# Bursts of the attention's small matmuls, 600 places ahead in the scheduler's order

## The chip, the core and the metric

The kernel runs on one core of a Trainium2 chip. The core has a matrix engine (PE, whose weight loads are listed apart as PEld), a vector engine (DVE), a scalar engine (ACT), GpSimd (POOL), and SyncE (SP), on whose queue most transfers are issued. Each engine works through its own instructions in their order, and they wait for each other through semaphores. The metric is the device time of one execution in microseconds (us); of several executions the median counts. The profile is of one further execution.

## The reference

Three parts follow each other: an attention over 4 batches of 8 heads (576 positions, 64 columns), a gated product of four weight matrices, and a mixture of 8 experts, of which each of the 2304 tokens uses one.

```python
q_d = q.reshape(B, H, Sd, 4, D).mean(axis=3)           # k_d, v_d likewise
out_up = np.repeat(sm_attn(q_d, k_d, v_d), 4, axis=2)
mask = np.abs(pos[:, None] - pos[None, :]) < 4
attn = softmax(where(mask, scale * q @ k.T, -1e9))
x = (out_up + attn @ v).transpose(0, 2, 1, 3).reshape(2304, 512)
...
h = (x @ w1) * (x @ w2) @ w3
x = h @ w_out
...
e_idx = argmax(x @ w_gate); h = maximum(x[mask] @ w1[e], 0); ye = h @ w2[e]
out[mask] = gate_w * sigmoid(x @ w_output_gate)[e] * ye
```

## The kernel before

**Stages.** First `w_out` and `w3` come in as 64-bit numbers, are unpacked to 32 bits by three DVE instructions for each block (`f64_bits`, lines 127 to 129) and multiplied with each other into `wc`, so that only one product follows the gated one. Then `w1` and `w2` are unpacked in the same way (`w_part`), and the tokens go through in six groups of 384: `g1_step` multiplies a group with a 128-column block of `w1` and of `w2` and forms the gated product, `g2_step` multiplies that with `wc`. From the third stage on the experts' products follow; their order on PE is written out by hand (`ordered`).

**Large products.** Each of them is made of three matmuls (`mm3`, lines 390 to 392), since every operand is split in a rounded high part and a remainder, and both are held in the type fp32r. Their moving operands have 256 to 384 columns here.

**The attention.** It is worked in 16 units, a pair of heads each, and has five steps for a unit:
- `a_T`: sums of four neighbours (`qz` on POOL, `kd` on DVE);
- `a_S1`: 24 matmuls of 32x64 (line 191) for the band of local scores and three of 96x144 (line 202, operand `kd`) for the coarse ones; DVE, POOL and ACT form the exponentials;
- `a_S2`: sums, reciprocals and scaling on DVE and POOL (`sm`, `ed`, `vd`);
- `a_V1`: a DVE transpose of `sm` (line 237), four ACT copies of it into `bd` (line 240), and six PE transposes of `ed` (line 245) that ACT copies into `pt`;
- `a_V2`: four matmuls with `pt` (line 256) and twelve with `bd` (line 260), then ACT and DVE add the results into `xr`, from which `x_split` makes `xh` and `xl` for `g1_step`.

The operands of these small matmuls are plain fp32. Each small matmul leaves two records in the trace, a transpose one. Their results go to three PSUM tiles that take turns (`at`).

**What sets the order.** `step(n)` takes the next n attention steps from a list (`side`), and the tables `GSTEP`, `W3STEP`, `G1STEP` and `G2STEP` say how many are taken after which product. All attention steps of a batch must be through before the group that reads them is split. The order in which instructions then stand on each engine is made by a scheduler: an instruction has a priority by its place in the program, and among those that it takes to be ready the one that stands earliest goes first. A step is written inside `tc.high_priority(offset=120)`, so all that it issues stands 120 places earlier than its place in the program:

```python
    def step(n=1):
        for _ in range(n):
            if side:
                fn, u = side.pop()
                with tc.high_priority(offset=120):
                    fn(u)
```

So a burst of small matmuls and the large products around it can stand at nearly the same priority and mix. The transfers for the next units (`a_load`, `a_loadk`, `a_loadd`, `a_loadv`) are issued on SP by `step` behind the steps that free their buffers.

Of the kernel before, what the change touches and what calls it, by code (L numbers as in the profile page):

```python
# [21 lines left out]
B, H, S, D = 4, 8, 576, 64  # L22
# [26 lines left out]
def attention_moe_kernel(ctx: ExitStack, tc: tile.TileContext, q, k, vw_in, v4_in, w1, w2, w3, w_out,  # L49
                         w_gate, w_ogate, e_w1, e_w2, out):  # L50
    nc = tc.nc
# [13 lines left out]
    def mt(shape, dt, name, tag=None, bufs=None):  # L65
        return main.tile(shape, dt, name=name, tag=tag or name, bufs=bufs)


    ident = mt([P, P], F32, "ident")
# [68 lines left out]
    def at(shape, dt, name, bufs=1):  # L138
        return att.tile(shape, dt, name=name, tag=name, bufs=bufs)

    kz = at([P, 2, 584], F32, "kz")
    qTs = [at([P, 584], F32, f"qT{i}") for i in range(2)]
    bd = at([P, 12, 96], F32, "bd")
# [2 lines left out]
        nc.gpsimd.memset(t, 0.0)  # L146
    st = {}

    def a_load(u):
        d = st.setdefault(u, {})  # L150
        qT = qTs[u % 2]
        kc = at([P, S], F32, "kc")
        nc.sync.dma_start(out=kc, in_=k[u])
        nc.sync.dma_start(out=qT[:, 0:S], in_=q[u])
        d.update(kc=kc, qT=qT)
# [28 lines left out]
    def a_S1(u):  # L184
        d = st[u]
        qT = d["qT"]
        ps = psa.tile([P, 512], F32, name="at", tag="at")
        sl = ps[:, 0:384].rearrange("p (b h k) -> p b h k", b=6, h=2)
        for g in range(24):
            b, j = divmod(g, 4)  # L190
            nc.tensor.matmul(sl[32 * j:32 * j + 32, b], qT[:, 24 * g:24 * g + 32], kz[:, :, 24 * g:24 * g + 32],  # L191
                             start=True, stop=True, tile_position=(0, 32 * j))
        sm = at([P, 6, 2, 32], F32, "sm", bufs=2)
        mx = at([P, 6, 2], F32, "mx")
        nc.vector.tensor_tensor(sm, sl, mask.unsqueeze(2).to_broadcast([P, 6, 2, 32]), op=ALU.add)
        nc.vector.tensor_reduce(out=mx, in_=sm, axis=AX.X, op=ALU.max)
        nc.gpsimd.tensor_tensor(sm, sm, mx.unsqueeze(3).to_broadcast([P, 6, 2, 32]), op=ALU.subtract)
        ps = psa.tile([P, 512], F32, name="at", tag="at")
        sd = ps[0:96, 0:432].rearrange("p (q k) -> p q k", q=3)
        qf = qz.rearrange("p h n -> p (h n)")  # L200
        for qb in range(3):
            nc.tensor.matmul(sd[:, qb], qf[:, 96 * qb:96 * qb + 96], d["kd"], start=True, stop=True)  # L202
        ed = at([96, 3, 144], F32, "ed", bufs=2)
        md = at([96, 3], F32, "md")
        nc.vector.tensor_reduce(out=md, in_=sd, axis=AX.X, op=ALU.max)
        nc.vector.tensor_scalar(md, md, -1.0 / 128, None, op0=ALU.mult)
        zd = at([96, 3], F32, "zd", bufs=2)
        nc.scalar.activation(out=sm, in_=sm, func=AF.Exp, scale=0.125)
        for qb in range(3):
            nc.scalar.activation(out=ed[:, qb], in_=sd[:, qb], func=AF.Exp, scale=1.0 / 128,  # L210
                                 bias=md[:, qb:qb + 1], accum_out=zd[:, qb:qb + 1])
        d.update(sm=sm, ed=ed, zd=zd)
# [20 lines left out]
    def a_V1(u):  # L233
        d = st[u]
        sm, ed = d["sm"], d["ed"]
        sT = at([P, 12, 32], F32, "sT")
        nc.vector.transpose(sT, sm.rearrange("p b h k -> p (b h) k"))
        for j in range(4):
            r = slice(32 * j, 32 * j + 32)
            nc.scalar.copy(out=bd[r, :, 24 * j:24 * j + 24], in_=sT[r, :, 0:24])  # L240
        pt = at([72, 2, 288], F32, "pt")
        for kb in range(2):
            pv = psa.tile([P, 512], F32, name="at", tag="at")
            for qb in range(3):
                nc.tensor.transpose(pv[0:72, 96 * qb:96 * qb + 96], ed[:, qb, 72 * kb:72 * kb + 72], ident[0:96, 0:96])  # L245
            nc.scalar.copy(out=pt[:, kb], in_=pv[0:72, 0:288])
        d["pt"] = pt

    def a_V2(u):
        d = st.pop(u)  # L250
        b, hp = divmod(u, H // 2)
        vw, vd, pt = d["vw"], d["vd"], d["pt"]
        xl = [psa.tile([P, 512], F32, name="at", tag="at") for _ in range(2)]
        for kb in range(2):
            for h in range(2):
                nc.tensor.matmul(xl[0][64 * h:64 * h + 64, 288:432], vd[:, kb, h, :], pt[:, kb, 144 * h:144 * h + 144],  # L256
                                 start=(kb == 0), stop=(kb == 1))
        for c in range(6):
            for h in range(2):
                nc.tensor.matmul(xl[c // 3][64 * h:64 * h + 64, 96 * (c % 3):96 * (c % 3) + 96], vw[:, c, D * h:D * h + D],  # L260
                                 bd[:, 2 * c + h, :], start=True, stop=True)
        up = at([P, 144], F32, "up")
        nc.scalar.copy(out=up, in_=xl[0][:, 288:432])
        for a in range(2):
            n = b * S + 288 * a
            assert G * split[0] >= n + 288 - RING
            o = 0
            while o < 288:
                r0 = (n + o) % RING
                w = min(288 - o, RING - r0)  # L270
                nc.vector.tensor_tensor(
                    xr[:, hp, r0:r0 + w].rearrange("p (n r) -> p n r", r=4), xl[a][:, o:o + w].rearrange("p (n r) -> p n r", r=4),
                    up[:, 72 * a + o // 4:72 * a + (o + w) // 4].unsqueeze(2).to_broadcast([P, w // 4, 4]), op=ALU.add)
                o += w
# [5 lines left out]
    for b in range(B):  # L280
        for s in range(UB + 4):
            for lag, fn in ((4, a_V2), (3, a_V1), (2, a_S2), (1, a_S1), (0, a_T)):
                if 0 <= s - lag < UB:
                    side.append((fn, b * UB + s - lag))
    side.reverse()
# [7 lines that stand above are left out]
                if fn is a_V1:  # L293
                    a_loadv(u)
                if fn is a_T and u + 1 < NU:
                    a_load(u + 1)
                if fn is a_S1:
                    if u + 1 < NU:
                        a_loadk(u + 1)
                    a_loadd(u)  # L300
# [580 lines left out]
    for n in range(4):  # L881
        f64_load("3", n)
        if n == 1:
            a_load(0)
            a_loadk(0)
# [212 lines left out]
```

## Time and profile before

| | us |
|---|---|
| three timed runs | 777.54, 775.76, 778.25 (median 777.54) |
| the profiled execution | 771.75 |
| its span, from the first to the last instruction | 769.9 |
| PE busy in the span | 739.4 |
| DVE busy in the span | 436.3 |
| POOL, ACT busy in the span | 322.9, 279.6 |

A busy share says how long an engine had something under way, not whether its work was dense. The records of PE overlap: a matmul's time runs from its start to its modelled end, while the next one has already begun, so its cost is read from start to start. Line numbers are those of the kernel before. The attention and the gated products fill the span up to about 480 us; the experts follow.

### The profile page before, as it was taken

How to read it: one execution, taken by the hardware profiler on the slowest of the kernel's cores; microseconds unless marked ns; L12 is line 12 of the kernel's file. 1: busy time of each engine (PE TensorE's matmuls, PEld its weight loads, DVE VectorE, ACT ScalarE, POOL GpSimd, SP SyncE). 2: the span in 40 equal slices, each digit the busy share in tenths (PEclk: the TensorE clock that was granted, in tenths of full speed). 3: DMA queues.
4: the chain of work that ended last, by engine and by line, in shares of the span. 5: the costliest groups of instructions: out<-in, count | busy, mean ns of one | idle time of the engine just before them, and what ended most of it. 6: DMA issues, size and time to landing. Idle time of an engine off the chain costs nothing.

```text
span 769.9 us, 14699 instructions
## 1 busy us (share of the span) xinstructions
PE 739.4 (96%) x5710; PEld 683.3 (89%) x5711; DVE 436.3 (57%) x940; ACT 279.6 (36%) x624; POOL 322.9 (42%) x306
## 2 busy tenths in 40 slices
PE   5789999999999999999999999989999999999995
PEld 3667987888978898899899999978999999999994
DVE  8977897962653254445324343455765566676731
ACT  3423534550233223323421212045443644544610
POOL 6744576852360125213201112035654656755611
PEclk9899999999999999999999999998999999999999
DMA  9994565542131313121110010256645447447301
GB/s 325 332 240 139 173 189 160 171 136 91 54 109 31 115 29 111 47 77 38 42 42 22 1 42 1 60 199 241 213 146 210 148 149 268 146 148 260 111 23 39
DMA packets 38264, 97.72 MB, mean 127 GB/s; under 512 B 6018, under 2 KB 12930, under 8 KB 38192
## 3 DMA queue, kind: packets, MB, share of 16 engines
q1 hardware_dynamic: 34768, 86.82, 35.1%
q0 software_dynamic: 3424, 9.93, 3.6%
q8 instruction: 46, 0.75, 0.4%
q14 instruction: 26, 0.21, 0.1%
HBM read 84.93 MB, written 12.29 MB: 126 GB/s over the span
## 4 chain that ended last, share of the span: by engine, by line
PE 86%; issue 5%; POOL 3%; DVE 3%; DMA 1%; ACT 1%; SPq 0%; POOLq 0%; ACTq 0%
PE g L390 24%; PE g L392 24%; PE g L391 23%; PE at L260 3%; PE at L191 3%; PE at L256 2%; PE at L202 2%; PE tr L686 1%; PE at L245 1%; PE tr L779 1%; POOL out_dram L769 1%; DMA early<-in_moe_w_dram 1%; PE g L322 1%; POOL W L713 1%; DVE wf L129 1%
## 5 line engine op out<-in xcount | busy, mean ns | idle before, releaser
L390 PE MATMUL g<-xh,W 128*128 128x384 f32 x384 | 133.8, 349 | 0.0
L392 PE MATMUL g<-xh,W 128*128 128x384 f32 x384 | 131.0, 342 | 0.0
L391 PE MATMUL g<-xl,W 128*128 128x384 f32 x384 | 130.8, 341 | 0.0
L713 DVE TENSOR_TENSOR W<-raw,W 128x1024 fp32r<-128x1024 f32 x32 | 87.9, 2780 | 32.2 <-ACT W L711 30.1
L713 POOL TENSOR_TENSOR W<-raw,W 128x1024 fp32r<-128x1024 f32 x29 | 82.8, 2879 | 37.0 <-ACT W L711 37.0
L390 PE MATMUL g<-xT,W 128*128 128x288 f32 (+6 forms) x256 | 82.2, 321 | 1.0 <-ACT xT L690 1.0
L391 PE MATMUL g<-xT,W 128*128 128x288 f32 (+6 forms) x256 | 80.2, 313 | 0.0
L392 PE MATMUL g<-xT,W 128*128 128x288 f32 (+6 forms) x256 | 80.0, 312 | 0.0
L423 POOL TENSOR_TENSOR h<-a,h 128x384 fp32r<-128x384 f32 x30 | 30.7, 1023 | 113.9 <-ACT h L421 113.7
L390 PEld LDWEIGHTS g<-xh,W 128*128 128x128 f32 x384 | 72.2, 188 | 3.2 <-issue 0.4
L392 PEld LDWEIGHTS g<-xh,W 128*128 128x128 f32 x384 | 72.1, 188 | 1.9 <-issue 0.4
L391 PEld LDWEIGHTS g<-xl,W 128*128 128x128 f32 x384 | 72.2, 188 | 1.5 <-issue 0.2
L390 PE MATMUL g<-wc,h 128*128 128x272 f32 (+1 forms) x240 | 70.2, 293 | 0.0
L391 PE MATMUL g<-wc,h 128*128 128x272 f32 (+1 forms) x240 | 70.0, 292 | 0.0
L390 PE MATMUL g<-h,W 128*128 128x288 f32 (+5 forms) x224 | 70.0, 312 | 0.0
L392 PE MATMUL g<-wc,h 128*128 128x272 f32 (+1 forms) x240 | 69.9, 292 | 0.0
L391 PE MATMUL g<-h,W 128*128 128x288 f32 (+5 forms) x224 | 68.1, 304 | 0.0
L392 PE MATMUL g<-h,W 128*128 128x288 f32 (+5 forms) x224 | 68.1, 304 | 0.0
L711 ACT CAST W<-raw 128x1024 fp32r<-128x1024 f32 x61 | 59.8, 1046 | 8.1 <-DMA raw<-in_moe_w_dram 4.3
L419 DVE TENSOR_TENSOR a<-g,a 128x384 f32<-128x384 f32 x48 | 26.7, 556 | 60.2 <-PE g L392 56.4
L739 ACT ACTIVATE h<-g 128x288 fp32r<-128x288 f32 (+6 forms) x64 | 27.9, 436 | 78.6 <-PE g L392 76.3
L390 PEld LDWEIGHTS g<-xT,W 128*128 128x128 f32 x256 | 49.1, 192 | 1.5 <-ACT xT L690 1.4
(255 smaller groups left out, 1721.8 us busy)
## 6 DMA issues: line engine op xcount, KB each, us to landing
raw<-in_moe_w_dram SPq DMA_DIRECT2D x61, 512.0 KB, 3.6
f64w<-in_moe_w_dram SPq DMA_DIRECT2D x16, 512.0 KB
f<-in_moe_w_dram SPq DMA_DIRECT2D x16, 512.0 KB, 6.5
vw<-in_vw_dram SPq DMA_DIRECT2D x16, 384.0 KB, 3.2
kc<-in_k_dram SPq DMA_DIRECT2D x16, 288.0 KB, 6.4
qT<-in_q_dram SPq DMA_DIRECT2D x16, 288.0 KB, 4.3
kz<-in_k_dram SPq DMA_DIRECT2D x32, 144.0 KB, 3.7
v<-in_v_dram SPq DMA_DIRECT2D x16, 288.0 KB
```

Of the source, the lines that this page charges most:

```text
L191: nc.tensor.matmul(sl[32 * j:32 * j + 32, b], qT[:, 24 * g:24 * g + 32], kz[:, :, 24 * g:24 * g + 32], start=True, stop=True, tile_positio ...
L202: nc.tensor.matmul(sd[:, qb], qf[:, 96 * qb:96 * qb + 96], d["kd"], start=True, stop=True)
L256: nc.tensor.matmul(xl[0][64 * h:64 * h + 64, 288:432], vd[:, kb, h, :], pt[:, kb, 144 * h:144 * h + 144], start=(kb == 0), stop=(kb == 1))
L260: nc.tensor.matmul(xl[c // 3][64 * h:64 * h + 64, 96 * (c % 3):96 * (c % 3) + 96], vw[:, c, D * h:D * h + D], bd[:, 2 * c + h, :], start=T ...
L390: nc.tensor.matmul(ps, whi, xhi, start=first, stop=False)
L391: nc.tensor.matmul(ps, whi, xlo, start=False, stop=False)
L392: return nc.tensor.matmul(ps, wlo, xhi, start=False, stop=last)
L419: nc.vector.tensor_tensor(a, pp[1][:, 0:G], a, op=ALU.mult)
L423: eng.tensor_tensor(lo, a, hi.bitcast(F32), op=ALU.subtract)
L711: nc.scalar.copy(out=hi, in_=t)
L713: ins = eng.tensor_tensor(lo, t, hi.bitcast(F32), op=ALU.subtract)
L739: return nc.scalar.activation(out=t[:, 0, 0:C], in_=ps[:, 0:C], func=AF.Relu), nc.vector.scalar_tensor_tensor(t[:, 1, 0:C], ps[:, 0:C], 0. ...
```

## The change

A context `burst()` is added that puts whatever is issued inside it 600 places further ahead. It is laid around the small matmuls of `a_S1` (both kinds), the transposes of `a_V1` and the matmuls of `a_V2`. The offset adds to the 120 of `step`. The matmuls themselves, their operands, the instructions on other engines and the tables are as before; but since the scheduler goes by what is ready, other instructions change places with them.

```diff
+    def burst():
+
+        return tc.high_priority(offset=600)
...
-        for g in range(24):
-            b, j = divmod(g, 4)
-            nc.tensor.matmul(sl[32 * j:32 * j + 32, b], qT[:, 24 * g:24 * g + 32], kz[:, :, 24 * g:24 * g + 32],
-                             start=True, stop=True, tile_position=(0, 32 * j))
+        with burst():
+            for g in range(24):
+                b, j = divmod(g, 4)
+                nc.tensor.matmul(sl[32 * j:32 * j + 32, b], qT[:, 24 * g:24 * g + 32], kz[:, :, 24 * g:24 * g + 32],
+                                 start=True, stop=True, tile_position=(0, 32 * j))
...
-        for qb in range(3):
-            nc.tensor.matmul(sd[:, qb], qf[:, 96 * qb:96 * qb + 96], d["kd"], start=True, stop=True)
+        with burst():
+            for qb in range(3):
+                nc.tensor.matmul(sd[:, qb], qf[:, 96 * qb:96 * qb + 96], d["kd"], start=True, stop=True)
...
-            for qb in range(3):
-                nc.tensor.transpose(pv[0:72, 96 * qb:96 * qb + 96], ed[:, qb, 72 * kb:72 * kb + 72], ident[0:96, 0:96])
+            with burst():
+                for qb in range(3):
+                    nc.tensor.transpose(pv[0:72, 96 * qb:96 * qb + 96], ed[:, qb, 72 * kb:72 * kb + 72], ident[0:96, 0:96])
...
+        with burst():
+            for kb in range(2):
+                for h in range(2):
+                    nc.tensor.matmul(xl[0][64 * h:64 * h + 64, 288:432], vd[:, kb, h, :], pt[:, kb, 144 * h:144 * h + 144],
+                                     start=(kb == 0), stop=(kb == 1))
+            for c in range(6):
+                for h in range(2):
+                    nc.tensor.matmul(xl[c // 3][64 * h:64 * h + 64, 96 * (c % 3):96 * (c % 3) + 96], vw[:, c, D * h:D * h + D],
+                                     bd[:, 2 * c + h, :], start=True, stop=True)
```

Four lines are added ahead of them and one at each burst, so lines 191, 202, 245, 256, 260 and 390 to 392 are 196, 208, 252, 264, 268 and 398 to 400 in the new file.

The order on PE in the second token group's gated products (`g_2772` to `g_2830`), where `a_V2` of the ninth unit stands. Before:

```order
L391 MATMUL g_2772<-xl,W_1618 128x384
L256 MATMUL at<-pt,vd 64x144
L392 MATMUL g_2772<-xh,W_1619 128x384
L256 MATMUL at<-pt,vd 64x144
L390 MATMUL g_2772<-xh,W_1618 128x384
L256 MATMUL at<-pt,vd 64x144
L391 MATMUL g_2772<-xl,W_1618 128x384
L256 MATMUL at<-pt,vd 64x144
L392 MATMUL g_2772<-xh,W_1619 128x384
L260 MATMUL at<-bd,vw 64x96
L390 MATMUL g_2772<-xh,W_1618 128x384
L260 MATMUL at<-bd,vw 64x96
```

Now, the same unit:

```order
L196 MATMUL at<-kz,qT_112 32x64 x13
L264 MATMUL at<-pt,vd 64x144 x4
L268 MATMUL at<-bd,vw 64x96 x6
L398 MATMUL g_2815<-xh,W_1797 128x384
...
L398 MATMUL g_2830<-xh,W_1806 128x384
L268 MATMUL at<-bd,vw 64x96 x6
L252 MATMUL at<-ident,ed 72x96 x6
```

The row before it went on in the same way: sixteen small matmuls stood in fifteen pieces, each behind a large one. Now they stand in two, the first behind another unit's `a_S1`, with nineteen large matmuls between the two.

The order on PE where `a_S1` of the sixth unit stands. Before, in the first group's gated products (`g_1469`):

```order
L191 MATMUL at<-kz,qT_113 32x64
L390 MATMUL g_1469<-xh,W_1356 128x384
L191 MATMUL at<-kz,qT_113 32x64
L391 MATMUL g_1469<-xl,W_1356 128x384
L191 MATMUL at<-kz,qT_113 32x64
L392 MATMUL g_1469<-xh,W_1357 128x384
```

Now, in the products that make `wc` (`g_1065`):

```order
L400 MATMUL g_1065<-wo,w3T 128x256
L196 MATMUL at<-kz,qT_113 32x64 x24
L398 MATMUL g_1065<-wo,w3T 128x256
L399 MATMUL g_1065<-wc,w3T 128x256
L400 MATMUL g_1065<-wo,w3T 128x256
```

The 24 matmuls are one piece, and the unit has moved ahead of the first gated product.

The order on DVE around the unpacking of one block of `w1` (`f_1365`; its `cv` and `wf` rows are `f64_bits`, the rows between them are attention and `wc`). Before:

```order
L127 TENSOR_SCALAR cv<-f_1365 128x512
L224 RECIPROCAL zd<-zd 96x3
L219 TENSOR_REDUCE su<-sm 128x12
L128 SCALAR_TENSOR_TENSOR cv<-f_1365,cv 128x512
L220 TENSOR_SCALAR su<-su 128x12
L221 RECIPROCAL su<-su 128x12
L355 TENSOR_TENSOR wc<-g_1302,wc 128x272
L237 STREAM_TRANSPOSE sT<-sm 128x384
L129 SCALAR_TENSOR_TENSOR wf<-f_1365,cv 128x512
```

Now, from the second of the three instructions on:

```order
L128 SCALAR_TENSOR_TENSOR cv<-f_1365,cv 128x512
L211 TENSOR_REDUCE md<-at 96x3
L200 TENSOR_TENSOR sm<-at,mask 128x384
L185 TENSOR_REDUCE kd<-kc 128x144
L243 STREAM_TRANSPOSE sT<-sm 128x384
L212 TENSOR_SCALAR md<-md 96x3
L201 TENSOR_REDUCE mx<-sm 128x12
L279 TENSOR_TENSOR xr<-at,up 128x192
L279 TENSOR_TENSOR xr<-at,up 128x96
L229 TENSOR_SCALAR zd<-zd 96x3
L230 RECIPROCAL zd<-zd 96x3
L129 SCALAR_TENSOR_TENSOR wf<-f_1365,cv 128x512
```

Ten rows of attention steps stand between the second and the third instruction of the block; before the last block's `wf` (`f_1735`) DVE had 287 rows, and now has 294.

## Rows read from the trace of the kernel before

**Rows 1.** The page's first part: busy us, share of the span, instructions.

```profile
PE 739.4 (96%) x5710; PEld 683.3 (89%) x5711; DVE 436.3 (57%) x940; ACT 279.6 (36%) x624; POOL 322.9 (42%) x306
```

**Rows 2.** Stretches: length, busy us of PE, PEld, DVE, ACT, POOL; clock, DMA share, GB/s.

```profile
40.00:160.00 120.00, 115.51 (x1058) 97.84 (x1057) 100.86 (x202) 54.17 (x148) 73.07 (x78) 1.00 0.62 182
130.00:160.00 30.00, 30.00 (x284) 25.22 (x283) 27.77 (x59) 16.80 (x46) 23.55 (x25) 1.00 0.65 193
160.00:480.00 320.00, 320.00 (x2481) 293.82 (x2480) 132.94 (x416) 94.06 (x249) 82.60 (x98) 1.00 0.18 55
```

**Rows 3.** PE in order of time, `a_V2` in series: start us, us, instruction, records.

```profile
221.00 0.46 PE L256 MATMUL at<-pt,vd 72*64 72x144 f32 x2
221.76 0.46 PE L256 MATMUL at<-pt,vd 72*64 72x144 f32 x2
...
224.05 0.38 PE L260 MATMUL at<-bd,vw 128*64 128x96 f32 x2
224.36 0.44 PE L390 MATMUL g<-xh,W 128*128 128x384 f32 x1
224.73 0.38 PE L260 MATMUL at<-bd,vw 128*64 128x96 f32 x2
```

**Rows 4.** PE in order of time, a burst in one piece; then pieces of the chain.

```profile
218.14 0.34 PE L392 MATMUL g<-xh,W 128*128 128x384 f32 x1
218.41 0.88 PE L191 MATMUL at<-kz,qT 128*32 128x64 f32 x48
219.21 0.98 PE L202 MATMUL at<-kd,qz 128*96 128x144 f32 x6
219.93 0.43 PE L390 MATMUL g<-xh,W 128*128 128x384 f32 x1
220.20 0.34 PE L391 MATMUL g<-xl,W 128*128 128x384 f32 x1
220.38 0.34 PE L392 MATMUL g<-xh,W 128*128 128x384 f32 x1
...
285.34 0.64 PE at L256 x8
285.99 0.99 PE at L260 x24
295.89 0.81 PE at L191 x48
```

**Rows 5.** PE in order of time, `a_S1` in series.

```profile
117.30 0.30 PE L191 MATMUL at<-kz,qT 128*32 128x64 f32 x2
117.89 0.30 PE L191 MATMUL at<-kz,qT 128*32 128x64 f32 x2
```

**Rows 6.** PE in order of time, the `kd` matmuls in series.

```profile
307.36 0.41 PE L202 MATMUL at<-kd,qz 128*96 128x144 f32 x2
307.78 0.41 PE L202 MATMUL at<-kd,qz 128*96 128x144 f32 x2
```

**Rows 7.** PE's waits from 30 to 200 us: in total, times, the longest.

```profile
PE g L390 <- DVE wc L355: 4.1, 2, 2.8
...
PE at L191 <- ACT w3T L341: 0.3, 1, 0.3
```

**Rows 8.** PEld in order of time, the same series as in rows 3.

```profile
221.00 0.19 PEld L256 LDWEIGHTS at<-pt,vd 72*64 72x64 f32 x2 [0.25 <-issue]
221.39 0.19 PEld L392 LDWEIGHTS g<-xh,W 128*128 128x128 f32 x1 [0.20 <-issue]
```

**Rows 9.** Line 129: duration in ns, least, median, most; first and last start.

```profile
L129 DVE SCALAR_TENSOR_TENSOR wf<-f,cv x16: 628/676/689, 98.0 to 160.4; 128x512 uint32<-128x512 uint32 x16
```

**Rows 10.** Groups of instructions: busy us, mean ns of one; idle time before.

```profile
L240 ACT COPY bd<-sT 32x288 f32<-32x288 f32 x64 | 27.5, 430 | 14.1 <-PE at L260 8.7 <-DVE zd L223 2.2 <-DVE sT L237 2.0
L237 DVE STREAM_TRANSPOSE sT<-sm 128x384 f32<-128x384 f32 x16 | 9.2, 574 | 11.6 <-POOL sm L222 7.9 <-ACT bd L240 3.7
L206 DVE TENSOR_SCALAR md<-md 96x3 f32<-96x3 f32 x16 | 6.5, 405 | 0.0
```

More of the change, by code (lines that the diff above doesn't have):

```diff
@@ L253, in a_V2 @@
         xl = [psa.tile([P, 512], F32, name="at", tag="at") for _ in range(2)]
[L254 to L261, printed above, removed]
+        with burst():
[7 more added lines that the diff above has]
+                                     bd[:, 2 * c + h, :], start=True, stop=True)
         up = at([P, 144], F32, "up")
```

## The prediction

> **What bounds the kernel now.** I read the busy shares first, then the stretches, then the order of work on PE inside one stretch. PE is busy 96% of the span [rows 1], and from 160 to 480 us it is busy in every microsecond, while DVE works 133 of the 320 us there [rows 2]. In that stretch a microsecond taken off PE is a microsecond off the end, until something else comes late. Between 40 and 160 us it is different: PE is busy 115.5 of 120 us, but DVE 100.9, and 27.8 of the last 30 [rows 2]. PE's waits there are few, 4.1 us for DVE's two `wc` writes the largest [rows 7]; still, DVE has little room.
>
> A busy PE can be a badly used one. Two large products of 384 columns follow each other in 0.17 us (220.20, 220.38) [rows 4]. Where the attention's small matmuls stand one by one between them, the step from one small matmul to the next, with one large product between, is 0.68 us for the `bd` matmuls of `a_V2` and 0.76 us for its `pt` matmuls [rows 3], and 0.59 us for those of `a_S1` [rows 5]. In one piece the same work is much cheaper. A small matmul leaves two records (x2), so 48 records are 24 matmuls: 0.81 us for `a_S1`, hence 0.034 each; 0.64 for four `pt` matmuls, 0.16 each; 0.99 for twelve `bd` matmuls, 0.083 each [rows 4]. That gap is what the change can take away.
>
> **What a small matmul costs when it stands alone.** The step in the series, less the large product (0.17), less its own time in one piece:
> - `bd`: 0.68 - 0.17 - 0.08 = 0.43 us;
> - `pt`: 0.76 - 0.17 - 0.16 = 0.43 us;
> - `a_S1`: 0.59 - 0.17 - 0.03 = 0.39 us;
> - the three `kd` matmuls: they take 0.72 us in one piece, 0.24 each (219.21 to 219.93) [rows 4], and the series has a step of 0.42 [rows 6], so 0.42 - 0.17 - 0.24 = 0.01 us, nothing.
>
> A burst that stands in one piece pays too, but once: the large product before it takes 0.27 instead of 0.17 (218.14 to 218.41), the one behind it 0.27 (219.93 to 220.20), so 0.2 us for a whole burst [rows 4].
>
> The weight loads show the mechanism. In a series PEld sits idle 0.2 us before each load, and the load starts at the same time as its matmul (221.00, 221.39) [rows 8]; when the kind changes, the next weights are not fetched behind the running product. The Trainium skill, "TensorE: Matmul & The Clock Gate", in "Part 2: What happens when you issue a matmul", says that PE pulls a weight load ahead of matmuls in flight, so that the next tile's weights load while this one runs. By that rule where the small matmuls stand would cost nothing, and the result would be the last rival's below; the rows say 0.4 us each, and I go by the rows.
>
> **The change, part by part.** No instruction is added or removed; only places change. In the order on PE I counted runs of small matmuls between large products. Before: 109 runs of a single matmul (44 of `a_S1`, 35 `bd`, 15 `pt`, 15 `kd`) and 52 longer ones. Now: 3 single runs, all `kd`, and 40 longer ones. So
> - `a_S1`: 44 x 0.39 = 17.2 us;
> - `bd` and `pt`: 50 x 0.43 = 21.5 us;
> - `kd`: 12 x 0.01, nothing;
> - longer runs: 12 fewer x 0.2 = 2.4 us;
> - runs of transposes alone fall from 27 to 14. No row prices them, so between nothing and the 0.2 us of a lone burst, 2.6 us; I take nothing, since a transpose is one record and not two, and keep 2.6 in the range.
>
> That is 41 us less work on PE. Not all of it is on the path. By their places in the trace, 36 of the 94 single runs of `a_S1` and `a_V2` lie between 40 and 160 us (20 and 16: 20 x 0.39 + 16 x 0.43 = 14.7 us) and 58 lie after (24 x 0.39 + 34 x 0.43 = 24.0 us). The 24 us count in full: PE is never idle there, and DVE, at 42% of that stretch, hides nothing that could come forward.
>
> The 14.7 us are where DVE is the cover that may go. DVE unpacks the weights three instructions at a time; the last of these ends at 160.4 + 0.7 us [rows 9], and PE's first gated products need them. In the new order DVE has 294 rows in front of that last write, against 287; the bursts move attention units 4 to 7 ahead of the weight blocks, so seven more rows, some 3 us at the 0.4 to 0.6 us that such rows last [rows 10]. DVE would have to do 100.9 + 3 = 104 us of work. The densest rate it has shown over 30 us is 27.8/30 = 0.926 [rows 2]: 104 / 0.926 = 112 us instead of 120. So that stretch gives 8 us, not 14.7; its ends are 0 (DVE's waits only change their place) and 14.7.
>
> Behind the bursts the rest of the engines follows. A burst that ends earlier lets ACT copy its PSUM tile sooner, so `kz`, `qT` and `kc` of the next unit are requested sooner on SP's queue; DMA is at 18% from 160 to 480 us [rows 2], so nothing there runs into a full queue. From about 480 us PE's rows are the same as before, and the weight streams of the experts hang on PE's progress, so the tail is only shifted.
>
> Sum: 24.0 + 8 + 2 (the longer runs) = 34 us. On the profiled execution's 771.75 us that is 737.8; the three timed runs have a median of 777.54, and I forecast **743.5 us** for the median, taking the same 34 us off.
>
> **The rivals.**
> 1. *DVE holds the first 160 us where they are.* PE's gain there turns into waits for `W`, `wc` and `xh`. For it: DVE at 27.8 of 30 us. Against: it was idle 19 of the 120 us. Gain 24: 753.5 us.
> 2. *DVE keeps up.* The waits that left it idle were mostly waits for the late bursts themselves, and all 41 us arrive: 736.5 us.
> 3. *PE waits in front of its bursts; the kernel is slower.* PE works strictly in its order. A burst that stands 600 places ahead of its large neighbours can come up before its inputs are there, and then the large products behind it wait, too. The dearest place is `a_V2`: its `bd` comes from one DVE transpose (0.57 us) and four ACT copies (4 x 0.43 us) [rows 10], 2.3 us in a row. If all 16 units pay that, 16 x 2.3 = 37 us is lost against 34 won: 780.5 us. It decides from 34/16 = 2.1 us a unit. Against it: PE's only wait for a small matmul in that stretch was 0.3 us [rows 7], the scheduler places a burst where it takes its inputs to be ready, and in the new order other work of PE, mostly large products, stands between a unit's transposes and its `a_V2`.
> 4. *The place costs nothing.* If a pair took 0.17 + 0.08 us wherever it stands, PE would do the same work in the same time: 777.5 us. The rows with 0.68 us speak against it; what speaks for it is only that matmul ends are modelled. But the steps are taken from starts.
>
> **How the numbers follow.** The forecast, with a gain of 28 to 38 us, gets 0.66; rival 1, with 20 to 28, 0.17; rival 2, 0.10; rival 3, 0.04; rival 4, 0.03. The range goes from rival 2's 736.5 to 757: the upper end takes 0.33 us for each of the 58 late single runs, about half way between the 0.2 us of a lone burst and the 0.43 of the series (19 us), and 1 us of the early gain. What can be told from no change in this kernel is about 0.3%, 2.3 us. Forecast, rivals 1 and 2 are all faster by more: 0.93. Rival 4 is the same: 0.03. Rival 3 is slower: 0.04.
>
> **What the new profile should show.** Between 160 us and the last attention unit, each `a_V2` in a few pieces at most, with `bd` records at about 0.04 us each where 24 stand together; the products from 160 to 480 us done in some 26 us less, at a PE that is still busy throughout; DVE's last unpacked block at 150 to 155 us instead of 161; DVE above 0.9 busy from 40 us to there, and some 6 us more of PE waits for DVE, ACT or POOL in that stretch; the part behind the attention as long as before. I am wrong if PE's waits in front of L256 to L260 (eight lines further down in the new file) add up to more than 10 us, or if large products next to bursts still take 0.4 us.

## The result, and the profile after

The changed kernel takes **744.1 us** (median of four runs, 739.9 to 746.7), the kernel before beside it 777.4: a ratio of 0.957, 95% interval 0.952 to 0.962. A second set of runs gave 743.5 and 0.959 (0.954 to 0.964). The forecast was 743.5, with 34 us gained; the medians differ by 33.3. The sum behind it did not hold in all its terms, though: the two profiled executions differ by 28.3 us only (771.75 and 743.41).

The page's first part answers [rows 1], the stretches answer [rows 2] (length, busy us of PE, PEld, DVE, ACT, POOL; clock, DMA share, GB/s):

```profile
PE 706.0 (95%) x5710; PEld 671.9 (91%) x5711; DVE 437.9 (59%) x940; ACT 280.3 (38%) x624; POOL 324.5 (44%) x306
```

```profile
40.00:80.00 40.00, 34.79 (x419) 31.07 (x419) 32.49 (x72) 19.00 (x58) 22.09 (x24) 0.96 0.80 220
80.00:120.00 40.00, 38.34 (x508) 35.29 (x507) 38.77 (x80) 20.01 (x58) 29.59 (x34) 1.00 0.64 185
40.00:160.00 120.00, 112.14 (x1201) 102.39 (x1201) 104.50 (x213) 59.62 (x163) 83.46 (x89) 0.99 0.68 199
160.00:480.00 320.00, 318.81 (x2621) 307.76 (x2620) 143.26 (x453) 94.57 (x246) 76.58 (x89) 1.00 0.19 58
```

PE was busy 739.4 us before and is busy 706.0 now, with the same 5710 instructions: 33.4 us of busy time are gone, and it is busy for 318.8 of the 320 us from 160 to 480 us. Between 40 and 160 us it is idle 7.9 us instead of 4.5, and DVE does more in that time (104.5 us against 100.9).

The ninth unit's `a_V2`, which stood one by one [rows 3], now stands in two pieces. That of the tenth, which stood one by one as well, is one piece (PE in order of time: start us, us, instruction, records):

```profile
229.47 0.28 PE L398 MATMUL g<-wc,h 128*128 128x272 f32 x1
229.59 0.29 PE L399 MATMUL g<-wc,h 128*128 128x272 f32 x1
229.81 0.71 PE L264 MATMUL at<-pt,vd 72*64 72x144 f32 x8
230.35 1.16 PE L268 MATMUL at<-bd,vw 128*64 128x96 f32 x24
231.44 0.39 PE L400 MATMUL g<-wc,h 128*128 128x272 f32 x1
231.67 0.29 PE L398 MATMUL g<-wc,h 128*128 128x272 f32 x1
```

All sixteen matmuls take 1.63 us from 229.81 to 231.44; the 24 `bd` records take 1.09 of it, 0.045 each. The large product before them takes 0.22 from start to start, the one behind them 0.23, where two in a row take 0.12. So this burst pays the 0.2 us of a piece once.

Three landmarks show where the time went. The first product of `h` with `wc` starts at 168.06 us before and at 163.21 now (PE in order of time; the first fence is of the kernel before):

```profile
167.88 0.34 PE L392 MATMUL g<-xh,W 128*128 128x384 f32 x1
168.06 0.29 PE L390 MATMUL g<-wc,h 128*128 128x272 f32 x1
...
465.16 0.33 PE L392 MATMUL g<-xh,W 128*128 128x384 f32 x1
```

```profile
163.03 0.34 PE L400 MATMUL g<-xh,W 128*128 128x384 f32 x1
163.21 0.29 PE L398 MATMUL g<-wc,h 128*128 128x272 f32 x1
...
436.93 0.33 PE L400 MATMUL g<-xh,W 128*128 128x384 f32 x1
```

That is 4.9 us for the stretch ahead of it in this pair of profiles. The 2091st large matmul (the last row of each fence), in the last gated products, starts at 465.2 before and 436.9 now, so 28.2 us are gained there, 23.4 of them between the two landmarks (297.1 us before, 273.7 now). Behind that point nothing more is gained: the last large matmul starts at 761.0 before and 732.8 now, 28.2 us. So the part behind the attention is only shifted, as forecast.

### The profile page after: what moved, and what is told of

Read it like the earlier page. It is cut to its first block, busy times and chain, and to the rows that moved or that the text cites. A ratio compares the mean times of both kernels' runs of the same rounds, so it can differ in the third digit from the quotient of the medians.

```text
span 741.7 us, 14714 instructions
## 1 busy us (share of the span) xinstructions
PE 706.0 (95%) x5710; PEld 671.9 (91%) x5711; DVE 437.9 (59%) x940; ACT 280.3 (38%) x624; POOL 324.5 (44%) x306
## 4 chain that ended last, share of the span: by engine, by line
PE 76%; DMA 7%; POOL 6%; issue 6%; DVE 4%; ACT 1%; SPq 0%; POOLq 0%; DVEq 0%; ACTq 0%
PE g L398 22%; PE g L399 21%; PE g L400 21%; DMA v<-in_v_dram 3%; PE at L268 2%; DMA vw<-in_vw_dram 2%; PE at L208 1%; PE at L196 1%; PE tr L694 1%; PE at L264 1%; PE tr L787 1%; PE g L330 1%; PE at L252 1%; POOL out_dram L777 1%; DMA early<-in_moe_w_dram 1%
## 5 line engine op out<-in xcount | busy, mean ns | idle before, releaser
L398 PE MATMUL g<-xh,W 128*128 128x384 f32 x384 | 131.0, 341 | 0.6 <-DVE a L427 0.5
L400 PE MATMUL g<-xh,W 128*128 128x384 f32 x384 | 129.8, 338 | 0.7 <-POOL W L377 0.6
L399 PE MATMUL g<-xl,W 128*128 128x384 f32 x384 | 129.3, 337 | 0.0
L399 PE MATMUL g<-wc,h 128*128 128x272 f32 (+1 forms) x240 | 68.2, 285 | 0.0
L398 PE MATMUL g<-wc,h 128*128 128x272 f32 (+1 forms) x240 | 68.2, 285 | 0.0
L400 PE MATMUL g<-wc,h 128*128 128x272 f32 (+1 forms) x240 | 67.8, 285 | 0.0
L777 POOL DMA_INDIRECT out_dram<-orow,b_si x24 | 23.5, 978 | 62.9 <-DVE orow L776 59.3
```

What stands on the lines that cost most here:

```text
L398: nc.tensor.matmul(ps, whi, xhi, start=first, stop=False)
L399: nc.tensor.matmul(ps, whi, xlo, start=False, stop=False)
L400: return nc.tensor.matmul(ps, wlo, xhi, start=False, stop=last)
L777: ins = nc.gpsimd.indirect_dma_start(out=out, out_offset=bass.IndirectOffsetOnAxis(ap=rt["si"][0:n, r, b:b + 1], axis=0), in_=t[0:n], in_o ...
```

## The experiments

All kernels are made from the changed one. In the first four and in the one with `a_S1` and `a_V2` alone, `burst` takes a flag, so that some of its four places can be taken back to `step`'s own priority:

```diff
-    def burst():
+    def burst(on=True):
 
-        return tc.high_priority(offset=600)
+        return tc.high_priority(offset=600) if on else nullcontext()
```

"Excess" below is read in the trace from start to start: what a run of small matmuls between two large ones takes, with the lengthening of the large ones on both sides, less what the same matmuls take in a long piece; a wait of PE beside such a run is counted in it. In the kernel before, up to 480 us, it is 17.2 us for 44 single `a_S1` matmuls (0.39 each), 15.0 for 35 `bd` (0.43), 6.0 for 15 `pt` (0.40), nothing for `kd`, and 16.8 for 46 longer runs.

**Only `a_S1` in a burst.** The other three places are `burst(False)`.

> Only the 24 small matmuls of a_S1 are issued 600 places ahead; the other bursts as in the kernel before. On PE this leaves no single a_S1 matmul between large products, against 44 before, but 64 single a_V2 matmuls (13 pt, 51 bd) instead of 50, since the rest of the order shifts. Theory (the price is 0.39 us for each a_S1 matmul alone and 0.43 us for each a_V2 matmul alone): PE's work falls by 44 x 0.39 - 14 x 0.43 = 11 us, some of it hidden by DVE before 160 us, so 6 to 11 us under the kernel before. Rival (what counts is that units come earlier, not that matmuls stand together): half of the change's 33 us, some 16 us or more, since a_S1 is the step that starts a unit's chain.

Measured: 761.6 us, ratio 0.982 (0.975 to 0.990). No single `a_S1` matmul is left, but there are more of the others, 51 `bd` and 13 `pt` (26.9 us against 21.0): what no longer hides between `a_S1` matmuls mixes with the large ones. By the prices -17.2 + 5.9 = -11.3 us, and the longer runs, which no price covers, cost 12.0 us instead of 16.8. The profiled executions differ by 11.3, the medians by 17.7, so by its total this run does not tell the price from the rival. The stretch between the two landmarks follows the price: it takes 283.2 us, 14.0 less than before, and 24 single `a_S1` and 9 single `bd` and `pt` fewer there are priced at 13.2.

**Only `a_V2` in a burst.** `a_S1`, `kd` and the transposes are `burst(False)`.

> Only the matmuls of a_V2 are issued 600 places ahead. On PE no single a_V2 matmul is left (50 before), and the 44 of a_S1 stay. Theory (the price per single): 50 x 0.43 = 21.5 us less PE work, 34 of the 50 after 160 us, so 15 to 21 us under the kernel before. Rival (earlier units): little, 0 to 8 us, since a_V2 is the last step of a unit and nothing of the unit follows it on PE.

Measured: 759.1 us, ratio 0.976 (0.970 to 0.980); the medians differ by 20.3 us, the profiled executions by 11.8. 44 single `a_S1` matmuls are left, at 0.40 us, as many as before the change; `bd` and `pt` have none. Between the landmarks it takes 281.0 us, 16.1 less than before, where 34 single `bd` and `pt` and one `a_S1` fewer are priced at 15.0. The rival had 0 to 8 us. So each of the two large terms is there by itself.

**Only `kd` and the transposes in bursts.** `a_S1` and `a_V2` are `burst(False)`.

> Only the three kd matmuls and the six transposes of a unit are issued 600 places ahead. On PE the single a_S1 matmuls rise from 44 to 63 and the single a_V2 matmuls from 50 to 67. Theory (the price per single): 19 x 0.39 + 17 x 0.43 = 14.7 us more PE work, so 8 to 15 us slower than the kernel before. Rival (earlier units): these bursts start the chains of ed and pt sooner, so faster than before by some us.

Measured: 811.9 us, ratio 1.045 (1.039 to 1.052): slower, and by more than twice what was expected. The trace shows `a_V2` in series at more places than before:

```profile
253.04 0.38 PE L268 MATMUL at<-bd,vw 128*64 128x96 f32 x2
253.35 0.44 PE L398 MATMUL g<-xh,W 128*128 128x384 f32 x1
253.73 0.38 PE L268 MATMUL at<-bd,vw 128*64 128x96 f32 x2
```

The step from one `bd` matmul to the next is again 0.69 us, with one large matmul in it. Single runs are 63 `a_S1`, 49 `bd` and 18 `pt`, 57.3 us against 38.2, and 60 longer runs cost 30.5 against 16.8: 19.1 + 13.7 = 32.8 us. The profiled execution's span is 804.2, 34.3 more than before. By count and price the singles account for 14.7 us of it, as was expected; 3.4 us more come from eight `bd` matmuls that stand between 59 and 73 us, where the granted clock was about 0.5, the 1.2 GHz level, and the longer runs had no price. So moving one kind ahead can break up the others, at more than twice what the count of singles says.

**Bursts in units 8 to 15 alone** (`burst(u >= 8)` at all places).

> All bursts are issued 600 places ahead in units 8 to 15 only; units 0 to 7 as in the kernel before. On PE the single matmuls fall from 94 to 46 (20 a_S1, 26 a_V2), and what stays lies before 160 us, where DVE is the fullest engine. Theory (each single of the late units counts in full, the early ones only in part): 24 x 0.39 + 24 x 0.43 = 19.7 us less PE work, all of it on the path, so 17 to 22 us under the kernel before, and 8 to 16 us over the changed kernel. Rival (DVE hides all that is won before 160 us): as fast as the changed kernel within 5 us.

Measured: 760.6 us, ratio 0.979 (0.974 to 0.984), 17 us above the changed kernel. The early stretch keeps its 40 single runs (four of them `kd`; 14.5 us of excess), and its landmark comes at 173.2 us, later than before though nothing was moved there (more on this below); from there to the 2091st large matmul it takes 278.4 us, against 297.1 before: 18.7 us. Of the late singles 12 are left (4.1 us), so 19.8 us were due. The late term arrives nearly in full where it is made alone.

**The price by itself.** Three kernels add 96 matmuls of 64x96 to the experts' products of three experts; their results are thrown away. In the first they stand behind every third large matmul, mostly one by one; in the second the same 96 stand in pieces of four; the third is the first with the operands read as fp32r, the type of the large products, instead of plain fp32.

```diff
+        def small(kk):
+            c = slice(256 * kk + P * (f % 2), 256 * kk + P * (f % 2) + 64)
+            nc.tensor.matmul(probe[0:64, 96 * kk:96 * kk + 96], hi[:, c].bitcast(F32), xT[r][0][:, kk, 0:96].bitcast(F32), start=True, stop=True)
...
+            if probe is not None:
+                with tc.issue_after(end.ins):
+                    small(kk)
```

> The changed kernel, with 96 extra small matmuls (64 by 96, plain fp32, results thrown away) among the first products of three experts, where PE is busy throughout and nothing else has changed: they stand in 60 runs between large products, 42 of them single, 9 double, 9 of four. Theory (a price for each time PE turns from fp32r to a small fp32 matmul and back): 60 runs at 0.4 us and 96 at their own 0.08 us, 32 us over the changed kernel. Rival (what made them dear in the attention was its own waits or its PSUM tiles): 96 x 0.08 = 8 us over it.

> The same 96 extra matmuls in 24 runs of four. Theory: 24 x 0.2 to 0.4 + 96 x 0.08 = 13 to 17 us over the changed kernel, 15 to 19 us under the run with 60 runs. Rival (own cost alone): 8 us over the changed kernel, as the run with 60 runs.

> The same 96 extra matmuls, spread in 45 runs (27 single), but with their operands read as fp32r, the type of the large products, from the same tiles. Theory A (the price is for the change of type): no price, only their own time, one record each at 0.04 to 0.08 us, 4 to 8 us over the changed kernel. Theory B (the price is for a small weight tile between large ones, whatever the type): 45 x 0.4 + 4 to 8 = 22 to 26 us.

> The changed kernel itself, as what the three others are held against on this chip: 740 to 747 us as in its own runs, 0.957 of the kernel before.

Measured on the same chip: the changed kernel 743.5 us, one by one 778.1, in pieces of four 766.5, one by one as fp32r 748.7. So the same 96 matmuls cost 34.5, 23.0 and 5.1 us. PE in order of time, first one by one, then in pieces, then as fp32r:

```profile
556.29 0.41 PE L398 MATMUL g<-xT,W 128*128 128x320 f32 x1
556.54 0.30 PE L399 MATMUL g<-xT,W 128*128 128x320 f32 x1
556.69 0.31 PE L400 MATMUL g<-xT,W 128*128 128x320 f32 x1
556.93 0.38 PE L741 MATMUL tr<-xT,W 128*64 128x96 f32 x2
557.24 0.41 PE L398 MATMUL g<-xT,W 128*128 128x320 f32 x1
```

```profile
556.77 0.31 PE L400 MATMUL g<-xT,W 128*128 128x320 f32 x1
557.00 0.87 PE L741 MATMUL tr<-xT,W 128*64 128x96 f32 x8
557.81 0.41 PE L398 MATMUL g<-xT,W 128*128 128x320 f32 x1
558.06 0.30 PE L399 MATMUL g<-xT,W 128*128 128x320 f32 x1
```

```profile
554.81 0.30 PE L400 MATMUL g<-xT,W 128*128 128x320 f32 x1
554.95 0.21 PE L741 MATMUL tr<-xT,W 128*64 128x96 f32 x1
554.99 0.38 PE L398 MATMUL g<-xT,W 128*128 128x320 f32 x1
555.21 0.31 PE L399 MATMUL g<-xT,W 128*128 128x320 f32 x1
```

Two large matmuls follow each other in 0.147 us here. One plain small matmul takes 0.31 us (556.93 to 557.24), the large one before it 0.24, the one behind it 0.25. As fp32r it takes 0.04, the large one before it 0.14, the one behind it 0.22. (The fp32r matmuls stand in 45 pieces, 27 of them single, the plain ones in 60.) Same shape, same places in the code, same operands: what costs is hardly the small shape, but that the matmul is plain fp32. Of the 29.4 us between the two, 96 x (0.165 - 0.044) = 11.6 are the matmuls' own time (worked out below); the other 18 are the turn between fp32r and plain fp32, in both directions. That turn is paid once for a piece, long or short: the large matmul before a piece of four takes 0.23 us and the one behind it 0.25, as with a single. This is the part of the price that a burst saves.

The pieces of four came out dearer than expected, by the matmul's own time: in one piece of four (eight records) it takes 0.81 us, 0.1 per record, and in the median 0.083 from record to record inside, so 0.165 for a matmul, where `bd` takes 0.083. The `bd` matmuls write two halves of the partitions in turn, these all the same; whether that is the reason is not shown. 96 x 0.165 = 15.9, and 24 pieces x 0.3 = 7.2, together 23.1 us.

**DVE's load.** The scaling of `md` goes to ACT.

```diff
-        nc.vector.tensor_scalar(md, md, -1.0 / 128, None, op0=ALU.mult)
+        nc.scalar.mul(md, md, -1.0 / 128)
```

> The changed kernel, with the scaling of `md` (16 instructions of 96x3, 0.405 us each on DVE, 6.5 us in all) moved from DVE to ACT. Theory A: DVE is what holds the early stretch of the changed kernel (102.4... of PE apart, DVE is at 104.5 of 120 us between 40 and 160, and at 38.8 of 40 between 80 and 120); some nine of the 16 fall before 160 us, 3.6 us of DVE, and the kernel should be 2 to 4 us faster than the changed one, 740 to 742 us. Rival: the early stretch is held by PE's own order and the transfers; then the time is that of the changed kernel within 1 us, 743 to 745.

Measured: 747.3 us, ratio 0.962 (0.958 to 0.966); neither of the two times expected, but some 3 us slower than the changed kernel. DVE had 11 instructions fewer between 40 and 160 us (202 against 213), but the last block was unpacked at 160.9 and the landmark came at 165.5. The edit also gives every engine another order, so it is no clean measure of DVE's share; it gives the theory that DVE's load holds the early stretch no support.

**`a_S1` and `a_V2` alone in bursts.** `kd` and the transposes are `burst(False)`.

> The changed kernel with the bursts around `a_S1`'s 24 matmuls and around `a_V2` alone; the `kd` matmuls and the transposes stand at their old priority. By the prediction's prices these two were worth nothing (0.01 us for a `kd` matmul, none for a transpose): the time should be that of the changed kernel, 742 to 746 us. Rival: whatever is left outside a burst mixes with the rest again, as it did where `kd` and transposes alone were bursts; then some 5 to 15 us slower, 749 to 759.

Measured: **740.5 us** (738.1 to 740.8), ratio 0.952 (0.948 to 0.957), profiled span 738.8 against 741.7. It is not slower, as the rival wanted, and 3 to 4 us under the changed kernel's medians; the intervals overlap, so "at least as fast" is what can be said. By the medians the gains of the two alone, 17.7 and 20.3 us, add up to 38.0, and both together give 36.5. No gain from the other two bursts shows.

**An offset of 60 in place of 600.**

> The changed kernel with an offset of 60 in place of 600. In the order on PE 60 single runs stand (29 of `a_S1`, 22 `bd`, 9 `pt`), against none of these in the changed kernel and 94 before. By the price of a single run, 29 x 0.39 + 31 x 0.43 = 24.6 us more work on PE than in the changed kernel, of 38.7 before: 24.6/38.7 of the 33 us, 21 us above the changed kernel, 762 to 768 us. Rival, that the distance matters and not the pieces (other engines' work comes earlier only with 600): as before the change, 775 to 780 us.

Measured: 768.2 us, ratio 0.990 (0.985 to 0.994). The trace has 29 single `a_S1` (11.5 us), 22 `bd` (9.5) and 9 `pt` (3.5): 24.5 us. The kernel is 24.7 us above the changed one. So the distance acts through the pieces that it leaves, and by their price, and not by itself: that rival had 775 to 780.

## Why the prediction was right, and where its steps were not

**The price of a single small matmul** (0.39, 0.43, 0.43 us): right. The same steps were read in every kernel that left some in series, and the time followed their count in both directions: 24.5 us in the trace against 24.7 in time with offset 60, and slower, not faster, with the bursts at the wrong places, though there the price covers 14.7 of the 34.3 us only. The price of nothing for `kd` and transposes held too.

**The late term** (24.0 us): right. From landmark to landmark 23.4 us are gained (23.2 to 23.7 in four further profiles with the same order there, the changed kernel again and the three with 96 matmuls added behind it), the excess of the late single runs falls from 23.9 us to nothing, and that of the longer runs from 6.4 to 7.3. Of the 23.4, 1.9 us is small work that has moved ahead of the first landmark.

**Longer runs** (12 fewer x 0.2 = 2.4 us gained, 2 in the sum): wrong in sign. They fell from 46 to 34 in the traces (52 to 40 by the count in the order), but their excess rose from 16.8 to 21.1 us. I priced a burst at 0.2 us from one good place; before, the mean was 0.37, now it is 0.62. Seven of the 34 take more than 1 us each, 11.7 together; the other 27 take 0.35. Part of what those seven take is waits:

```profile
PE at L264 <- ACT pt L253: 2.1, 1, 2.1
PE at L208 <- POOL qz L183: 1.3, 2, 0.9
...
PE at L196 <- DMA kz<-in_k_dram: 1.0, 1, 1.0
...
PE at L268 <- DMA vw<-in_vw_dram: 0.6, 2, 0.4
```

(PE's waits from 30 to 480 us: in total, times, the longest; [rows 7] had 0.3 us of this kind.) This is rival 3 in small: PE stands in front of a burst whose inputs are not there. With 0.2 us more at one `kd` burst it adds up to 5.2 us. Of these 2.7 are in front of `a_V2`, under the 10 that I had set there as the point where I would be wrong, and far from the 2.1 us a unit that would have undone the gain.

**The early term** (8 of 14.7 us): too high by this pair of profiles, but not by a second trace of the old order; and what cost the rest is not what I gave as the reason. The early single runs are gone (14.6 us to 0.0), the longer early runs cost 13.8 instead of 10.4 us, and only 4.9 us arrive; counting the small work that is done ahead of the landmark now and was not before, 6.8. One of the waits cost more than its length. PE in order of time, and then stretches (columns as above):

```profile
71.49 0.28 PE L400 MATMUL g<-wo,w3T 128*128 128x256 f32 x1
73.82 0.47 PE L264 MATMUL at<-pt,vd 72*64 72x144 f32 x4 [2.05 <-ACT pt L253]
74.67 0.72 PE L268 MATMUL at<-bd,vw 128*64 128x96 f32 x12 [0.38 <-DMA vw<-in_vw_dram]
...
76.58 1.18 PE L268 MATMUL at<-bd,vw 128*64 128x96 f32 x12
```

```profile
71.50:74.00 2.50, 0.45 (x7) 0.24 (x5) 2.22 (x7) 2.50 (x9) 0.04 (x1) 1.00 0.76 185
74.00:76.00 2.00, 1.62 (x20) 1.12 (x18) 0.83 (x2) 0.33 (x2) 2.00 (x2) 0.98 0.60 241
76.00:78.00 2.00, 2.00 (x18) 1.73 (x18) 0.59 (x2) 0.15 (x1) 2.00 (x3) 0.50 0.03 8
78.00:80.00 2.00, 2.00 (x13) 1.96 (x13) 1.97 (x5) 1.90 (x6) 0.94 (x2) 0.67 0.27 27
```

An early `a_V2` waits 2.05 us for a copy by ACT, and 0.38 for a transfer. PE is busy 0.45 of 2.5 us; behind that, from 76 us, the granted clock is 0.50, the 1.2 GHz level, until past 79 us, and twelve `bd` records that had taken 0.72 us take 1.18. Against full clock the last two stretches lack 2 x 0.50 + 2 x 0.33 = 1.7 us, so the place costs about 4 us where the wait was 2.4. In the four further profiles of this order the same `a_V2` waits 1.7 to 3.5 us for that copy. Over the 12 us from 68 to 80 the clock is 0.72 and 0.86 where that wait is 3.5 and 3.4 us, and 1.00 where it is 1.8; where it is 1.7 the clock is 0.86, but there it fell ahead of it, behind a wait of 1.9 us for `vw`. So the waits belong to the new order, and half clock came with them in four profiles of five.

The old order has a second trace, too. With bursts in units 8 to 15 alone, PE, DVE, ACT and POOL have the same instructions in the same order as in the kernel before up to 205 us, and yet the landmark comes 5.1 us later. PE in order of time and one stretch, first in the kernel before, then in that one:

```profile
19.52 1.06 PE L322 MATMUL g<-wot,wg 128*32 128x128 f32 x8 [0.73 <-ACT wot L320]
44.57 0.39 PE L390 MATMUL g<-wo,w3T 128*128 128x256 f32 x1 [2.82 <-DVE wc L355]
46.00:53.00 7.00, 6.74 (x97) 6.45 (x96) 5.41 (x13) 2.33 (x8) 1.88 (x2) 1.00 1.00 230
```

```profile
22.11 1.92 PE L330 MATMUL g<-wot,wg 128*32 128x128 f32 x8 [0.73 <-ACT wot L328]
47.58 0.58 PE L398 MATMUL g<-wo,w3T 128*128 128x256 f32 x1 [2.33 <-DVE wc L363]
46.00:53.00 7.00, 5.42 (x25) 5.42 (x26) 6.02 (x14) 3.62 (x12) 4.75 (x6) 0.52 0.93 257
173.15 0.29 PE L398 MATMUL g<-wc,h 128*128 128x272 f32 x1
```

At the same place, behind the same wait, the clock stayed at 1.00 in one execution and fell to 0.52 in the other; in the first 25 us, too, the same eight matmuls take 1.06 us in one and 1.92 in the other. From 53 us on the two keep their distance. So the old order's early stretch took 168.1 us in one execution and 173.2 in another, the new one's 161.8 to 164.7 in five. The early gain is 4.9 us against the one trace and 10.0 against the other; the 8 lies between, and that it was too high is not shown. Why the clock differs between executions is not shown either.

My mechanism for the early stretch was DVE. It does become dense, 38.8 of 40 us between 80 and 120 us, but over 120 us it did 104.5 us of work, not 104 in 112, and its last block came late:

```profile
L129 DVE SCALAR_TENSOR_TENSOR wf<-f,cv x16: 671/687/689, 102.2 to 158.6; 128x512 uint32<-128x512 uint32 x16
```

DVE was 0.87 busy from 40 to 160 us, not above 0.9, and PE's idle time there grew by 3.4 us, not by 6. The last block's write starts at 158.6, 1.8 us earlier than in [rows 9], where I had expected 150 to 155 for its end. But PE's waits for DVE's `wc` are 2.6 us where they were 4.1, so the lateness did not reach PE as a wait for DVE, and easing DVE's load gained nothing. DVE as the cap is not shown; what is shown is that bursts wait early, and that half clock mostly came with one such wait. Where DVE is fuller still, in the kernel with two bursts (39.7 of 40 us from 80 to 120), PE does wait 7.5 us for `wc`; there the cap begins to show.

**The sum** was 24 + 8 + 2 = 34. The two first traces say 23.4 + 4.9 = 28.3, with nothing for the longer runs by themselves; the medians say 33.3. The profiled execution of the kernel before is 5.7 us under its median, that of the changed kernel 0.7 under its own; I took the sum from the trace and laid it on the median. With the second trace of the old order the sum is 23.4 + 10.0 = 33.4, close to the medians, so the first one looks like a short execution, and its early stretch is where it was short. Short and long executions differ in their clock: of 31 timed executions of the kernel before in the experiments' sets, the eight with the highest mean granted clock (0.988 to 0.990) have a median of 773.0 us, the eight with the lowest (0.975 to 0.980) 779.3. That the forecast came out within 1 us is luck in part: the 2 us for the longer runs did not come, and the early stretch gave by the medians about 2 us more than the 8.

**The rivals.** That the place costs nothing (777.5) fell with the first result; that all 41 us arrive (736.5) fell, too, by the early stretch and the longer runs. That DVE holds the early 160 us (753.5) gave too little; that PE waits in front of its bursts is real, at 5.2 us of waits and the 1.7 us of clock behind one of them.

## What to carry to other kernels

Where matmuls of two types share a TensorE, read the step from start to start, not the busy share: a small plain fp32 matmul alone between fp32r products cost 0.4 us on top of its own 0.03 to 0.16 (and nothing where it took 0.24 by itself), and putting them together gives that back. Read as fp32r, the 96 added matmuls cost next to nothing beyond their own time; whether the attention's results would bear that type was not tried. Move all the kinds that mix, and count pieces in the new order: moving one kind ahead alone can break up the others and cost more than before. A burst that goes ahead of its neighbours must have its inputs: each early wait costs its own length, and here mostly a stretch at half clock as well. And one profile is one execution: where two gains differ by some us, look at the granted clock of both, stretch by stretch, before a term is called wrong.

## What the runs showed of the hardware

- **The turn between fp32r and plain fp32 is not hidden.** 60 pieces of plain small matmuls (96 in all) cost 34.5 us, the same matmuls as fp32r, in 45 pieces, 5.1; about 12 of the difference are the matmuls' own time, the rest the turn. In the trace, the large matmul ahead of a plain one takes 0.24 instead of 0.147 us, and the one behind it 0.25. The Trainium skill, "TensorE: Matmul & The Clock Gate", in "Part 2: What happens when you issue a matmul", has PE pull weight loads ahead of matmuls in flight; for fp32r neighbours the step of 0.04 us agrees with that, for a change of type it does not.
- **A plain fp32 matmul took nearly four times as long as an fp32r one.** 0.165 us against 0.044 for the same 96 columns, as added to the experts' products (the attention's `bd` matmuls of that shape take 0.083). The Trainium skill, "FP8 and Floating Point Precision", "TensorE Precision Notes", says that true fp32 makes four passes; the trace shows two records of 0.083 us each, which agrees in the time.
- **Transposes pay nearly nothing.** 14 runs of transposes alone have 2.8 us of excess in the changed kernel, 2.6 of it in one beside PE's wait of 2.3 us for `wc`, and 13 in the kernel with only `kd` and transposes ahead 0.3. A plain fp32 `kd` matmul of 96x144 takes 0.24 us in a piece and no more alone; why the turn does not show there is open.
- **Half clock came behind a wait in one execution and not in another, and also without a wait.** After the wait of 2.05 us the granted clock was 0.98, 0.50 and 0.67 in three stretches of 2 us, and 1.00 again from 80 us on. Behind the same wait for `wc` in the same order of work it stayed at 1.00 in the kernel before (2.82 us of waiting) and was 0.52 from 46 to 53 us in the kernel with late bursts (2.33 us). In the kernel with only `kd` and transposes ahead it was about 0.5 for 14 us in which PE was never idle, in and behind a series of single `bd` matmuls; the series of [rows 3] ran at 1.00.

```profile
59.00:73.00 14.00, 14.00 (x50) 9.47 (x49) 5.88 (x15) 3.79 (x9) 4.79 (x7) 0.51 0.31 98
```
